# A chunked retention followed by a bilinear layer: the first tile's output by seven products for eight, and a new order of supply

## The chip, the cores and the metric

The kernel runs on one core of one Trainium2 chip. The metric is the device time of one execution in microseconds, and less is better. Engines are named as in the profile: PE (TensorE, matmul), DVE (VectorE), ACT (ScalarE), POOL (GpSimd) and SP (SyncE, which here issues nearly all transfers). L561 is line 561 of the kernel.

## The reference

```python
# q, k, v: [4, 8, 768, 64] float32; w_a, w_b: [512, 1536]; w_out: [1536, 512]
gamma = 1.0 - 2.0 ** (-5.0 - np.arange(H))
state = zeros(B, H, D, D)
for t in range(S):
    state = gamma * state + einsum('bhd,bhe->bhde', k[:, :, t], v[:, :, t])
    y[:, :, t] = (1 / sqrt(D)) * einsum('bhd,bhde->bhe', q[:, :, t], state)
x = y.transpose(0, 2, 1, 3).reshape(3072, 512)
out = ((x @ w_a) * (x @ w_b)) @ w_out          # [3072, 512] float32
```

So an attention without softmax, with a decay per head, feeds a layer with two input matrices, a product of their results, and an output matrix.

## The kernel before

**Slots.** The 4 x 768 tokens are cut into 24 chunks of 128 tokens, called slots 0 to 23. For each slot K, Q and V of all 8 heads are loaded as float32 (`load_slot`, L94; `load_two`, L99, brings Q of two slots at once), K and Q are scaled by a decay table into bfloat16 (`scaled`, L239), V is cast (`cast`, L204 and L206), and K and Q are transposed by a DMA that writes kqT (L254). `casts(t)` does all of this for slot t on POOL, with the transpose and the loads of slot t + 2 issued behind it on SP; for slots 12 to 19 V is cast by ACT (`v_cast`). The raw tiles kf, qf, vf have three buffers each, kqT has three. Slots 0 to 5 go two at a time in another form (`scores2`, `inter2`, `intra2`, `leave2`) and are transposed by PE (`tp`, L375). `turn(new, old)` computes scores, state and output of two slots and writes the layer's input xt.

**Tiles.** The layer works on tiles of 4, 2, 2, 2, 2, 4 and 8 slots (0 to 6; tile 6 is called BIG). For a tile J and one of 12 blocks ft of 128 hidden columns, `ffn_ab(J, ft)` computes a (L462) and g (L472) on PE; ACT copies a, and DVE multiplies (L474) into `ht`. The banks of PSUM for this (`psff`, tag "ff") are three.

**Output, two forms.** `ffn_out` takes one row of 128 tokens: 12 matmuls of 512 columns (L493). It is used for the four rows of tile 0 alone. All other tiles use `Group`: two rows of tokens by the two halves of the 512 output columns, as 2 x 2 blocks, with seven block products in place of eight (p1 to p7, each six matmuls of 256 columns, L561). For it one needs four sums of `ht` (`hsum(J, s, a, b)`: sum s = 1 to 4, columns a to b of six) and four of the output weights (T1 to T4, `weight_sums`). Sum 2 uses sum 3, and sum 4 uses sum 2; p6 uses sum 2, p7 sum 3, p5 sum 1, p3 sum 4. All sums are L503, whichever engine does them. `single(J)` runs the group of tile J with the first three blocks of tile J + 1 between its products: p1 p7 p2, block 0, p6, block 1, p5, block 2, p3 p4. Tile 6 also takes its a and g by seven products, for which `weight_pieces` makes sums of w_a and w_b in small pieces on POOL.

**Order.** Every instruction goes through `seq`, which keeps each engine in the order of the program text. The order is written out by hand at the end of the kernel; nothing is planned by a tool. A wait of one instruction therefore holds all that follows on its engine and on its DMA queue. `LOADS` gives the order of the first loads: pairs of slots (p), weights a and b (w), K, Q and V of the third pair, the output weights (o), and then whole slots (s).

The program up to the first group, and the third and fifth stage, shortened:

```python
    casts(6); blocks(1, 0, 3); casts(7); blocks(1, 3, NFT)
    outs(0, 0); weight_sums(0, 3); weight_sums(3, 6); outs(0, 1); casts(8); outs(0, 2)
...
    hsums(3, 0, 3, G_); casts(15); blocks(3, 9, 10); turn(12, 10); blocks(3, 10, NFT)
    hsums(3, 3, 6, G_); casts(16); single(3, Y0, AT0, FF); casts(17)
...
    casts(22); blocks(5, 6, 9); casts(23); weight_pieces(1); turn(20, 18); sums(5, 8, G_)
    blocks(5, 9, NFT); turn(22, 20); sums(5, NFT - 1, G_); weight_pieces(16); big()
```

Of the kernel before, what the change touches and what calls it, by code (L numbers as in the profile page):

```python
# [9 lines left out]
F32 = mybir.dt.float32  # L10
BF16 = mybir.dt.bfloat16
AF = mybir.ActivationFunctionType
ALU = mybir.AluOpType
# [3 lines left out]
PAIRS = 3  # L17


LOADS = "p0 p1 w0 w1 w2 w3 w4 k2 q2 a5 v2 b5 o0 o1 o2 o3 o4 o5 s6 s7".split()  # L20


@with_exitstack
def kernel(
# [55 lines left out]

    raws, wst, whole = {}, {}, {}

    def load_slot(t):
        b, ci = divmod(t, NCH)
        for nm, src in (("k", k), ("q", q), ("v", v)):
# [8 lines left out]
            seq(nc.sync.dma_start(out=raws[nm, t], in_=s))  # L94

    def load_two(nm, src, b, u, t):
        f = raw.tile([P, H, 2, D], F32, tag=nm + "f", name=nm + "f")
# [26 lines left out]
    def issue_loads(n):  # L124
        for _ in range(min(n, len(pending))):
            what = pending.pop(0)
            n = int(what[1:])
            if what[0] in "ab":
                load_w(n, what[0])
            elif what[0] in "kqv":  # L130
                load_two(what[0], {"k": k, "q": q, "v": v}[what[0]], 0, n, 2 * n)
            else:
                {"p": load_pair, "s": load_slot, "w": load_w, "o": load_o}[what[0]](n)


    kqb = {}
# [65 lines left out]
    def cast(engine, dst, src):  # L202
        if engine is nc.scalar:
            seq(nc.scalar.copy(dst, src))  # L204
        else:
            seq(engine.tensor_copy(dst, src))  # L206

    def cast_w(j, names="ab"):
        sl = slice(j * WC, (j + 1) * WC)
        for nm, dst in (("a", wa_bf), ("b", wb_bf)):  # L210
            if nm in names:
                cast(nc.gpsimd, dst[:, :, sl], wst[nm, j])

    def cast_o(j):
        cast(nc.gpsimd, wo_bf[:, j * FPO : (j + 1) * FPO, :], wst["o", j])
# [30 lines left out]
    def casts(t):  # L246
        new_nat(t)
        scaled(nc.gpsimd, t, 0)
        scaled(nc.gpsimd, t, 1)
        if t not in range(12, 20):  # L250
            cast(nc.gpsimd, vb[t], raws["v", t])
        if t % 2 == 0:
            kqT[t // 2] = tra.tile([P, 2, 2, HP, P], BF16, tag="kqT", name="kqT", bufs=3)
        seq(nc.sync.dma_start_transpose(  # L254
            out=kqT[t // 2][:, t % 2].rearrange("p a b c -> p (a b) c"),
            in_=kqb[t].rearrange("p a hp r d -> p (a hp r d)")))
        if t + 2 < NSLOT:
            load_slot(t + 2)

    def half(i):  # L260
        return slice(64 * i, 64 * i + 64)
# [183 lines left out]
    def warm(pool, tag, *cols):  # L445
        idle = pool.tile([P, HP * P], F32, tag=tag, name="idle")
        for n in cols:
            seq(nc.tensor.matmul(idle[:, :n], zero[:, :P], zero[:, :n], start=True, stop=True,  # L448
                                 skip_group_check=True))
# [30 lines left out]

    held = []

    def store():
        for dst, src in held:
            seq(nc.sync.dma_start(out=dst, in_=src))
        held.clear()

    def ffn_out(J, i):
        store()
        osb = osbp.tile([P, DM], F32, tag="osb", name="osb")  # L490
        o = psff.tile([P, DM], F32, tag="ff", name="o")
        for ft in range(NFT):
            seq(nc.tensor.matmul(o, ht[J][:, ft, i * P : (i + 1) * P], wo_bf[:, ft],  # L493
                                 start=(ft == 0), stop=(ft == NFT - 1)))
        cast(nc.scalar, osb, o)
        held.append((rows(J, i // 2, i % 2), osb))

    def rows(J, u, r):
        n0 = (sum(TILES[:J]) + 2 * u) * P
        return out[n0 : n0 + 2 * P, :].rearrange("(n r) d -> r n d", r=2)[r]  # L500

    def tt(dst, x, y, op, eng=nc.vector):
        seq(eng.tensor_tensor(dst, x, y, op=op))  # L503

    T1 = []

    def weight_sums(a, b):
        if not T1:
            T1.append(wstage.tile([P, NP, DH], BF16, tag="w", name="wsum1"))
        j = slice(a, b)  # L510
        tt(T3[:, j], B22[:, j], B12[:, j], ALU.subtract)
        tt(T2[:, j], T3[:, j], B11[:, j], ALU.add)
        tt(T4[:, j], B21[:, j], T2[:, j], ALU.subtract)
        tt(T1[0][:, j], B12[:, j], B11[:, j], ALU.subtract)

    hs = {}

    def hsum(J, s, a, b, eng=nc.vector):
        U = 2 if isinstance(J, tuple) else TILES[J] // 2
        if (J, s) not in hs:  # L520
            pool, tag = (raw, ("kf", "qf", "vf", "kf")[s - 1]) if J == (BIG, 1) else (wstage, "w")
            hs[J, s] = pool.tile([P, NP, 2, P], BF16, tag=tag, name=f"hs{s}")
        v = ht[J].rearrange("p (k j) (u r n) -> p r k j u n", k=2, r=2, n=P)
        A11, A12, A21, A22 = (v[:, r, k2, a:b, :U] for r in range(2) for k2 in range(2))
        S = {x: hs[J, x][:, a:b, :U] for x in (1, 2, 3, 4) if (J, x) in hs}
        x, y, op = {3: (A11, A21, ALU.subtract), 2: (A22, S[3], ALU.subtract), 1: (A21, A22, ALU.add),
                    4: (A12, S.get(2), ALU.subtract)}[s]
        tt(S[s], x, y, op, eng)

    def hsums(J, a, b, eng):  # L530
        for s in (2, 1, 4):
            hsum(J, s, a, b, eng)
# [300 lines left out]
    ffn_a(0, 0, 0, W2)  # L833
    intra2(1, 1, False)
    leave2(1, (A_, D_))
    ffn_a(0, 1, 0, W2)
    issue_loads(100)
    cast_w(1)
    update2(1, 1)
    ffn_a(0, 0, W2, 2 * W2)  # L840
    ffn_a(0, 1, W2, 2 * W2)
    ffn_g(0, 0, 0, W2)
# [25 lines left out]
    intra2(2, 1, False)  # L868
    leave2(2, (A_, D_))
    ffn_g(0, 10)  # L870
    ffn_g(0, 11)
    for j in range(NO):
# [12 lines left out]
    def outs(J, *rows):  # L885
        for i in rows:
            ffn_out(J, i)
# [51 lines left out]
    v_cast(14)  # L939
    blocks(4, 3, 5)  # L940
    v_cast(15)
    blocks(4, 5, 6)
    turn(14, 12)
    hsum(4, 3, 0, 6, G_)
    blocks(4, 6, 8)
    v_cast(16)
    blocks(4, 8, 9)
    hsums(4, 0, 3, G_)
    casts(18)
    blocks(4, 9, 10)  # L950
    v_cast(17)
    blocks(4, 10, 11)
    turn(16, 14)
    blocks(4, 11, NFT)
    hsums(4, 3, 6, G_)
    casts(19)
    single(4, Y0, AT0, FF)
    casts(20)
# [12 lines left out]
    sums(5, 8, G_)  # L971
    blocks(5, 9, NFT)
    turn(22, 20)
    sums(5, NFT - 1, G_)
    weight_pieces(16)
    big()


# [28 lines left out]
```

## Time and profile before

| what | value |
|---|---|
| time, median of 3 runs | 222.55 us (222.44 to 222.66) |
| the profiled execution | 222.53 us |
| its span | 220.8 us |
| PE busy | 214.2 us (97%) |
| POOL busy | 140.6 us (64%) |
| DVE busy | 135.8 us (61%) |
| ACT busy | 99.2 us (45%) |
| bytes moved by DMA | 39.68 MB |

The span is what the hardware profiler recorded between the first and the last instruction; the 1.73 us beside it lie around it. A row of a timeline gives start and length in microseconds, engine, line, operation, the tile written and the tiles read, their shape, and how many instructions the row holds; brackets give the idle time before it and what ended it. SPq stands for the DMA queue's issues on SP; a row of it is the time for which the issue held the queue. Durations of matmuls overlap the next by a little, since their ends are modelled, so products are timed here from start to start.

### The profile page before, as it was taken

The page shows a single profiled execution, that of the slowest core. Times are in us where ns is not written, and L with a number is a line of the kernel's source. Part 1 is how long each engine was busy: PE and PEld are TensorE (multiplying, and loading weights), DVE is VectorE, ACT ScalarE, POOL GpSimd, SP SyncE. Part 2 cuts the span into 40 slices and gives each one's busy share as a digit, 9 for nine tenths or more (in the row PEclk, how much of TensorE's full clock was granted, in tenths as well). Part 3 has the DMA queues.
Part 4 walks back from the last instruction along what each step waited for, and adds up shares of the span by engine and source line. Part 5 has one row for each costly group of instructions (what it writes and reads, how often), then busy time and mean ns, then how long its engine had stood idle before and what let it go on. Part 6 is the DMA issues. An engine that isn't in the chain of part 4 may idle for free.

```text
span 220.8 us, 5622 instructions
## 1 busy us (share of the span) xinstructions
PE 214.2 (97%) x2233; PEld 144.6 (66%) x2244; DVE 135.8 (61%) x254; ACT 99.2 (45%) x217; POOL 140.6 (64%) x155
## 2 busy tenths in 40 slices
PE   7999999999999999999999999999999999999994
PEld 3567445587458878878888665456865444448883
DVE  3785347745774473566476345776465777789642
ACT  3364333443224444354576344555536656542331
POOL 5364666777554469659846944599999999820000
PEclk9999999999999999999999999999999999999999
DMA  6999999997999999999998599990022000000055
GB/s 170 290 324 348 350 309 342 385 262 164 217 186 286 214 239 240 237 180 274 188 224 219 118 245 194 225 174 3 3 85 105 0 1 3 0 1 4 24 190 166
DMA packets 87194, 39.68 MB, mean 180 GB/s; under 512 B 57472, under 2 KB 82944, under 8 KB 87168
## 3 DMA queue, kind: packets, MB, share of 16 engines
q1 hardware_dynamic: 87024, 39.26, 76.9%
q8 instruction: 17, 0.28, 0.5%
q14 instruction: 9, 0.07, 0.1%
q10 hardware_dynamic: 144, 0.07, 0.1%
HBM read 28.31 MB, written 6.29 MB: 157 GB/s over the span
## 4 chain that ended last, share of the span: by engine, by line
PE 93%; DMA 2%; DVE 2%; issue 1%; ACT 0%; SPq 0%; DVEq 0%; ACTq 0%
PE a L462 19%; PE g L472 19%; PE mA L561 12%; PE uA L698 8%; PE mB L561 6%; PE o L493 5%; PE uB L698 4%; PE mC L561 3%; DMA qf<-in_q_dram 2%; PE at L273 2%; PE y L320 2%; PE uC L698 2%; PE st L290 2%; PE kb L756 2%; PE ka L756 2%; PE y L427 1%
## 5 line engine op out<-in xcount | busy, mean ns | idle before, releaser
L474 DVE TENSOR_TENSOR ht<-g,asb 128x256 bf16<-128x256 f32 (+1 forms) x74 | 37.1, 503 | 40.4 <-PE g L472 34.0
L472 PE MATMUL g<-xt,wb_bf 128*128 128x256 bf16 (+1 forms) x296 | 53.2, 304 | 0.4 <-DVE ht L474 0.4
L462 PE MATMUL a<-xt,wa_bf 128*128 128x256 bf16 (+1 forms) x292 | 53.4, 304 | 0.2
L465 ACT CAST asb<-a 128x256 bf16<-128x256 f32 (+1 forms) x74 | 32.2, 437 | 44.6 <-PE a L462 42.0
L472 PEld LDWEIGHTS <-wb_bf 128*128 128x128 bf16 x296 | 28.8, 98 | 13.4 <-issue 0.7
L239 POOL TENSOR_TENSOR kqb<-kf,ktab 128x512 bf16<-128x512 f32 x22 | 23.2, 1057 | 20.4 <-DMA kf<-in_k_dram 17.3
L462 PEld LDWEIGHTS <-wa_bf 128*128 128x128 bf16 x296 | 27.9, 98 | 12.2 <-issue 0.8
L561 PEld LDWEIGHTS <-hs 128*128 128x128 bf16 x240 | 23.4, 98 | 3.9
L279 DVE TENSOR_TENSOR aT<-at,mask 128x512 bf16<-128x512 f32 x36 | 22.3, 683 | 0.3
L704 ACT COPY snap<-uA 128x512 f32<-128x512 f32 x30 | 16.7, 588 | 12.6 <-PE uA L698 12.0
L239 POOL TENSOR_TENSOR kqb<-qf,qtab 128x512 bf16<-128x512 f32 x18 | 19.2, 1066 | 4.7 <-DMA qf<-in_q_dram 4.7
L503 POOL TENSOR_TENSOR hs<-ht,hs 128x384 bf16<-128x384 bf16 (+1 forms) x17 | 16.6, 982 | 5.8 <-DVE ht L474 5.8
L568 ACT COPY snaps<-mA 128x256 f32<-128x256 f32 x30 | 11.2, 373 | 19.8 <-PE mA L561 19.7
L561 PEld LDWEIGHTS <-ht 128*128 128x128 bf16 x180 | 17.5, 98 | 2.8
L503 POOL TENSOR_TENSOR hs<-ht 128x384 bf16<-128x384 bf16 (+2 forms) x12 | 13.8, 1152 | 3.7 <-DVE ht L474 3.7
L561 PE MATMUL mA<-wsum,hs 128*128 128x256 bf16 x120 | 15.7, 273 | 0.0
L206 POOL CAST vb<-vf 128x512 bf16<-128x512 f32 x16 | 10.1, 643 | 7.3 <-DMA vf<-in_v_dram 7.1
L503 POOL TENSOR_TENSOR ht<-gsb,asb 128x512 bf16<-128x512 bf16 x12 | 13.9, 1169 | 1.3 <-DVE gsb L503 1.3
L503 DVE TENSOR_TENSOR osb<-mB,snaps 128x256 f32<-128x256 f32 x20 | 8.4, 422 | 9.4 <-PE mB L561 5.1
L493 PE MATMUL o<-wo_bf,ht 128*128 128x512 bf16 x46 | 10.6, 380 | 0.1
L331 ACT CAST xt<-y 128x512 bf16<-128x512 f32 x18 | 9.7, 588 | 1.5 <-PE y L320 1.4
L448 PE MATMUL idle<-zero 128*128 128x256 f32 (+2 forms) x16 | 8.2, 632 | 1.6 <-DVE zero L140 1.5
(104 smaller groups left out, 323.0 us busy)
## 6 DMA issues: line engine op xcount, KB each, us to landing
qf<-in_q_dram SPq DMA_DIRECT2D x12, 512.0 KB, 5.7
out_dram<-osb SPq DMA_DIRECT2D x21, 256.0 KB, 3.9
kf<-in_k_dram SPq DMA_DIRECT2D x18, 256.0 KB, 4.6
vf<-in_v_dram SPq DMA_DIRECT2D x18, 256.0 KB, 5.4
wsta<-in_moe_w_a_dram SPq DMA_DIRECT2D x6, 512.0 KB, 8.4
wstb<-in_moe_w_b_dram SPq DMA_DIRECT2D x6, 512.0 KB, 8.1
wsto<-in_moe_w_out_dram SPq DMA_DIRECT2D x6, 512.0 KB, 7.6
kf<-in_k_dram SPq DMA_DIRECT2D x3, 512.0 KB, 7.1
```

What stands on the lines that cost most here:

```text
L239: seq(eng.tensor_tensor(dst, src, tab, op=ALU.mult))
L279: seq(nc.vector.tensor_tensor(aT[t][:, r], at[r], mask.to_broadcast([P, HP, P]), op=ALU.mult))
L462: seq(nc.tensor.matmul(a, wa_bf[:, kt, fs], xcols(J, kt, c0, c1), start=(kt == 0), stop=(kt == KT - 1)))
L465: seq(nc.scalar.copy(asb, a))
L472: seq(nc.tensor.matmul(g, wb_bf[:, kt, fs], xcols(J, kt, c0, c1), start=(kt == 0), stop=(kt == KT - 1)))
L474: seq(nc.vector.tensor_tensor(ht[J][:, ft, c0:c1], g, asbs.pop((J, ft, c0)), op=ALU.mult))
L493: seq(nc.tensor.matmul(o, ht[J][:, ft, i * P : (i + 1) * P], wo_bf[:, ft], start=(ft == 0), stop=(ft == NFT - 1)))
L503: seq(eng.tensor_tensor(dst, x, y, op=op))
L561: seq(nc.tensor.matmul(m, w, right[:, j], start=(first and j == 0), stop=(j == NP - 1), skip_group_check=True))
L568: seq(nc.scalar.copy(self.snaps[:, n], self.bank["A"]))
L698: seq(nc.tensor.matmul(m, w, right[:, k], start=(first and k == 0), stop=(k == 1), skip_group_check=True))
L704: seq(nc.scalar.copy(self.snaps[n], self.bank["A"]))
```

## The change

- Tile 0's output is taken by two `Group`s, interleaved with each other, in place of four `ffn_out`. The sums of tile 0's `ht` are made on DVE in pieces of two of six columns: some behind blocks 5, 6, 8, 10 and 11 of tile 0, and 18 parts (`todo`), of `ht` and of the weights, one behind each of the blocks 0 to 8 of tile 1 and the rest between the groups' products. The buffers are raw tiles of kf, qf and vf, and one of kqT. The groups now stand between block 8 and block 9 of tile 1.
- Sum 3 and half of sum 2 of tile 1 move to POOL.
- The start: two half blocks of a of tile 0 in place of matmuls on zeros; the casts of the first two weight pieces come in halves; state update and first g block come earlier.
- Loads: output weights in the order in which the groups use them; slots 6 and 7 as k6, q6, k7, v6, v7. `casts_two(6)` scales and transposes both slots before it casts V, and the loads of 8 and 9 follow together.
- From slot 15 on, casts stand earlier among the sums on POOL: casts(15) ahead of the first three sums of tile 3, casts(17) between sum 2 and sum 1 of its second half; in the same way 18, 19, 20 for tile 4.
- Twelve weight pieces stand ahead of casts(22) and casts(23), four ahead of the sums of tile 5, eight behind them; the pieces are in a new order.

```diff
-LOADS = "p0 p1 w0 w1 w2 w3 w4 k2 q2 a5 v2 b5 o0 o1 o2 o3 o4 o5 s6 s7".split()
+LOADS = "p0 p1 w0 w1 w2 w3 w4 k2 q2 a5 v2 b5 o0 o3 o1 o4 o2 o5 s6".split()
...
+    def load_slots(t):
+        for u, names in ((t, "kq"), (t + 1, "k"), (t, "v"), (t + 1, "v")):
+            load_slot(u, names)
...
+    def casts_two(t):
+        for u in (t, t + 1):
+            new_nat(u)
+            scaled(nc.gpsimd, u, 0)
+            scaled(nc.gpsimd, u, 1)
+            flip(u)
+        for u in (t, t + 1):
+            cast(nc.gpsimd, vb[u], raws["v", u])
+        load_slots(t + 2)
...
-    for a, b in ((0, 1), (1, 3), (3, 5)):
-        pieces += [(w, n, a, b) for w, n in (("a", 3), ("a", 2), ("b", 3), ("b", 2), ("a", 1), ("b", 1),
-                                             ("a", 4), ("b", 4))]
+    FIRST = [("a", 3), ("a", 2), ("b", 3), ("b", 2), ("a", 1), ("b", 1)]
+    LAST = [("a", 4), ("b", 4)]
+    for cols, sums_of in (((0, 1), FIRST), ((1, 3), FIRST), ((0, 1), LAST), ((1, 3), LAST),
+                          ((3, 5), FIRST + LAST)):
+        pieces += [(w, n, *cols) for w, n in sums_of]
...
-    cast_w(0)
+    cast_w(0, parts=2)
     W2 = 2 * P
-    warm(psff, "ff", 256)
+    ffn_a(0, 0, 0, W2)
+    ffn_a(0, 1, 0, W2)
...
+        if ft in (5, 6):
+            hsum(0, 3, 2 * ft - 10, 2 * ft - 8)
+        if ft == 8:
+            hsum(0, 3, 4, 6)
+            hsum(0, 2, 0, 2)
...
     ffn_g(0, 10)
+    hsum(0, 2, 2, 4)
+    hsum(0, 1, 0, 2)
     ffn_g(0, 11)
+    hsum(0, 4, 0, 2)
...
-    casts(6)
-    blocks(1, 0, 3)
-    casts(7)
-    blocks(1, 3, NFT)
-    outs(0, 0)
-    weight_sums(0, 3)
-    weight_sums(3, 6)
-    outs(0, 1)
+    todo = ("S224 T302 S124 T324 T202 T346 T224 T246 T102 T124 T146 S246 S146 S424 S446 "
+            "T402 T424 T446").split()
...
+    casts_two(6)
+    for ft in range(9):
+        ffn_ab(1, ft)
+        part()
+    hsum(1, 3, 0, 6, G_)
+    hsum(1, 2, 0, 3, G_)
+    g = [Group(0, 0, Y0, AT0, FF), Group(0, 1, Y1, AT1, FF)]
+    for x in "a1 - - b1 - - a2 - a7 - a6 - b6 - b7 - a5 b5 b2 a3 b3 a4 b4".split():
+        if x == "-":
+            part()
+        else:
+            getattr(g["ab".index(x[0])], "p" + x[1])()
     casts(8)
-    outs(0, 2)
-    turn(6, None, V_)
-    hsum(1, 3, 0, 6)
-    hsums(1, 0, 6, V_)
-    outs(0, 3)
+    store(2)
+    turn(6, None)
+    for ft in range(9, NFT):
+        ffn_a(1, ft)
+    for ft in range(9, NFT):
+        ffn_g(1, ft)
+    hsum(1, 1, 0, 3)
+    hsum(1, 4, 0, 3)
     casts(9)
     turn(None, 6)
+    hsums(1, 3, 6, V_)
     single(1, AT0, AT1, FF)
...
+    casts(15)
     hsums(3, 0, 3, G_)
-    casts(15)
     blocks(3, 9, 10)
     turn(12, 10)
     blocks(3, 10, NFT)
-    hsums(3, 3, 6, G_)
     casts(16)
+    hsum(3, 2, 3, 6, G_)
+    casts(17)
+    hsum(3, 1, 3, 6, G_)
+    hsum(3, 4, 3, 6, G_)
     single(3, Y0, AT0, FF)
-    casts(17)
...
     v_cast(19)
+    weight_pieces(12)
     blocks(5, 5, 6)
     turn(18, 16)
     sums(5, 5)
     casts(22)
+    casts(23)
     blocks(5, 6, 9)
-    casts(23)
-    weight_pieces(1)
+    weight_pieces(4)
     turn(20, 18)
     sums(5, 8, G_)
     blocks(5, 9, NFT)
     turn(22, 20)
     sums(5, NFT - 1, G_)
-    weight_pieces(16)
+    weight_pieces(8)
     big()
```

More of the change, by code (lines that the diff above doesn't have):

```diff
@@ L81, with load_slot @@
     raws, wst, whole = {}, {}, {}
-    def load_slot(t):
+    def load_slot(t, names="kqv"):
         b, ci = divmod(t, NCH)
-        for nm, src in (("k", k), ("q", q), ("v", v)):
+        for nm in names:
+            src = {"k": k, "q": q, "v": v}[nm]
             if nm == "q":
@@ L132, in issue_loads @@
             else:
-                {"p": load_pair, "s": load_slot, "w": load_w, "o": load_o}[what[0]](n)
+                {"p": load_pair, "s": load_slots, "w": load_w, "o": load_o}[what[0]](n)
     kqb = {}
@@ L206, in cast, with cast_w @@
             seq(engine.tensor_copy(dst, src))
-    def cast_w(j, names="ab"):
-        sl = slice(j * WC, (j + 1) * WC)
+    def cast_w(j, names="ab", parts=1):
+        n = WC // parts
         for nm, dst in (("a", wa_bf), ("b", wb_bf)):
-            if nm in names:
-                cast(nc.gpsimd, dst[:, :, sl], wst[nm, j])
+            for i in range(parts if nm in names else 0):
+                c = j * WC + i * n
+                cast(nc.gpsimd, dst[:, :, c : c + n], wst[nm, j][:, :, i * n : (i + 1) * n])
     def cast_o(j):
@@ L251, in casts, with flip @@
             cast(nc.gpsimd, vb[t], raws["v", t])
+        flip(t)
+        if t + 2 < NSLOT:
+            load_slot(t + 2)
+    def flip(t):
         if t % 2 == 0:
@@ L256, in casts @@
             in_=kqb[t].rearrange("p a hp r d -> p (a hp r d)")))
-        if t + 2 < NSLOT:
-            load_slot(t + 2)
+    def casts_two(t):
[7 more added lines that the diff above has]
+        load_slots(t + 2)
     def half(i):
@@ L481, with store @@
     held = []
-    def store():
-        for dst, src in held:
+    def store(n=None):
+        for dst, src in held[:n]:
             seq(nc.sync.dma_start(out=dst, in_=src))
[L486 to L496, printed above, removed]
+        del held[:n]
     def rows(J, u, r):
@@ L505, with weight_sum @@
     T1 = []
-    def weight_sums(a, b):
-        if not T1:
+    def weight_sum(n, a, b):
+        if n == 1 and not T1:
             T1.append(wstage.tile([P, NP, DH], BF16, tag="w", name="wsum1"))
         j = slice(a, b)
[L511 to L514, printed above, removed]
+        x, y, op = {3: (B22, B12, ALU.subtract), 2: (T3, B11, ALU.add), 4: (B21, T2, ALU.subtract),
+                    1: (B12, B11, ALU.subtract)}[n]
+        tt({1: T1[0] if T1 else None, 2: T2, 3: T3, 4: T4}[n][:, j], x[:, j], y[:, j], op)
     hs = {}
@@ L520, in hsum @@
         if (J, s) not in hs:
-            pool, tag = (raw, ("kf", "qf", "vf", "kf")[s - 1]) if J == (BIG, 1) else (wstage, "w")
-            hs[J, s] = pool.tile([P, NP, 2, P], BF16, tag=tag, name=f"hs{s}")
+            pool, tag = (raw, ("kf", "qf", "vf", "kf")[s - 1]) if J in (0, (BIG, 1)) else (wstage, "w")
+            if (J, s) == (0, 4):
+                pool, tag = tra, "kqT"
+            bufs = {"bufs": 3} if pool is tra else {}
+            hs[J, s] = pool.tile([P, NP, 2, P], BF16, tag=tag, name=f"hs{s}", **bufs)
         v = ht[J].rearrange("p (k j) (u r n) -> p r k j u n", k=2, r=2, n=P)
@@ L827 @@
     update2(1, 0)
-    cast_w(0)
+    cast_w(0, parts=2)
     W2 = 2 * P
-    warm(psff, "ff", 256)
+    ffn_a(0, 0, 0, W2)
+    ffn_a(0, 1, 0, W2)
     intra2(1, 0, True)
     inter2(1)
-    ffn_a(0, 0, 0, W2)
     intra2(1, 1, False)
     leave2(1, (A_, D_))
-    ffn_a(0, 1, 0, W2)
+    update2(1, 1)
+    ffn_g(0, 0, 0, W2)
     issue_loads(100)
-    cast_w(1)
-    update2(1, 1)
+    cast_w(1, parts=2)
     ffn_a(0, 0, W2, 2 * W2)
     ffn_a(0, 1, W2, 2 * W2)
-    ffn_g(0, 0, 0, W2)
     ffn_g(0, 1, 0, W2)
@@ L870 @@
     ffn_g(0, 10)
+    hsum(0, 2, 2, 4)
+    hsum(0, 1, 0, 2)
     ffn_g(0, 11)
-    for j in range(NO):
+    hsum(0, 4, 0, 2)
+    for j in (0, 3, 1, 4, 2, 5):
         cast_o(j)
@@ L883, in v_cast, with part @@
         cast(nc.scalar, vb[t], raws["v", t])
-    def outs(J, *rows):
-        for i in rows:
-            ffn_out(J, i)
-    casts(6)
-    blocks(1, 0, 3)
-    casts(7)
-    blocks(1, 3, NFT)
-    outs(0, 0)
-    weight_sums(0, 3)
-    weight_sums(3, 6)
-    outs(0, 1)
-    casts(8)
-    outs(0, 2)
-    turn(6, None, V_)
-    hsum(1, 3, 0, 6)
-    hsums(1, 0, 6, V_)
-    outs(0, 3)
+    todo = ("S224 T302 S124 T324 T202 T346 T224 T246 T102 T124 T146 S246 S146 S424 S446 "
+            "T402 T424 T446").split()
+    def part():
+        what = todo.pop(0)
+        n, x, y = map(int, what[1:])
+        if what[0] == "S":
+            hsum(0, n, x, y)
+        else:
+            weight_sum(n, x, y)
+    casts_two(6)
[8 more added lines that the diff above has]
+            part()
+        else:
+            getattr(g["ab".index(x[0])], "p" + x[1])()
+    casts(8)
+    store(2)
[6 more added lines that the diff above has]
+    hsum(1, 4, 0, 3)
     casts(9)
     turn(None, 6)
+    hsums(1, 3, 6, V_)
     single(1, AT0, AT1, FF)
@@ L943 @@
     turn(14, 12)
+    casts(18)
     hsum(4, 3, 0, 6, G_)
@@ L946 @@
     v_cast(16)
+    casts(19)
     blocks(4, 8, 9)
     hsums(4, 0, 3, G_)
-    casts(18)
     blocks(4, 9, 10)
@@ L954 @@
     blocks(4, 11, NFT)
-    hsums(4, 3, 6, G_)
-    casts(19)
+    hsum(4, 2, 3, 6, G_)
+    casts(20)
+    hsum(4, 1, 3, 6, G_)
+    hsum(4, 4, 3, 6, G_)
     single(4, Y0, AT0, FF)
-    casts(20)
     v_cast(18)
```

## The prediction

> **What bounds the kernel now.** I read the page first, then what TensorE waits for, then single stretches of each engine's timeline. The page's lines:
>
> ```profile
> span 220.8 us, 5622 instructions
> ...
> PE 214.2 (97%) x2233; PEld 144.6 (66%) x2244; DVE 135.8 (61%) x254; ACT 99.2 (45%) x217; POOL 140.6 (64%) x155
> ...
> PEclk9999999999999999999999999999999999999999
> DMA  6999999997999999999998599990022000000055
> ```
>
> TensorE is busy for 97% of the span at full granted clock. Two things follow. Fewer matmul columns are worth their full time. And there is no slack for any new wait of TensorE: it lengthens the span by its own size. The DMA row shows the other resource that is full: from 5 us to about 115 us the sixteen engines are nearly always busy. The waits of TensorE in the whole execution (us in total, times, longest) are:
>
> ```profile
> PE idle L448 <- DVE zero L140: 1.5, 1, 1.5
> PE tp L375 <- DVE kqb L239: 0.5, 2, 0.3
> PE g L472 <- DVE ht L474: 0.4, 1, 0.4
> ```
>
> So little is there to be won from waits (2.4 us, of which 1.5 us is the start). The change must win by columns, and it can lose by every operand that comes late.
>
> **Tile 0's output.** Four rows of 12 products of 512 columns become two groups of 7 x 6 products of 256 columns (TensorE's timeline: start, us, what):
>
> ```profile
> 53.73 7.93 PE L493 MATMUL o<-wo_bf,ht 128*128 128x512 bf16 x35
> 61.59 0.32 PE L290 MATMUL st<-vb,kqb 128*64 128x64 bf16 x8
> 62.77 2.76 PE L493 MATMUL o<-wo_bf,ht 128*128 128x512 bf16 x11
> 65.46 0.31 PE L310 MATMUL y<-kqT,gst 64*64 64x128 bf16 x8
> 66.27 0.83 PE L561 MATMUL mA<-wo_bf,ht 128*128 128x256 bf16 x6
> 66.93 0.82 PE L561 MATMUL mB<-wsum,hs 128*128 128x256 bf16 x6
> ```
>
> The old form takes 61.59 - 53.73 = 7.86 and 65.46 - 62.77 = 2.69, together 10.55 us. A group of six products starts 0.66 after the one before it (66.27, 66.93), so 14 of them take 9.2 us. Saved: **1.4 us**. That is all the change can gain on TensorE in this part; everything else is waiting moved about.
>
> **The sums for it.** The groups need four sums of tile 0's hidden values and four of the weights; all go to VectorE, a part of them after the last blocks of tile 0, the others one after each block of tile 1. The rows of VectorE in those places, two of TensorE, and the same shape of sum later on:
>
> ```profile
> 36.29 0.69 DVE L206 COPY kqT<-tp 128x1024 bf16<-128x1024 bf16 x1
> 37.25 0.64 PE L384 MATMUL at<-kqT 64*64 64x128 bf16 x32
> 43.38 0.69 DVE L474 TENSOR_TENSOR ht<-g,asb 128x512 bf16<-128x512 f32 x1 [0.17 <-PE g L472]
> 44.13 0.60 PE L462 MATMUL a<-xt,wa_bf 128*128 128x256 bf16 x4
> 139.40 0.41 DVE L503 TENSOR_TENSOR hs<-ht 128x512 bf16<-128x512 bf16 x1
> 140.58 0.53 DVE L503 TENSOR_TENSOR hs<-ht 128x512 bf16<-128x512 bf16 x1
> ```
>
> A sum of 128x512 is 0.41 to 0.53. Two of them now stand ahead of the copy of kqT (36.29), behind the product of block 8. The copy ends at 36.98 now and 0.8 to 1.1 later then; the scores at 37.25 have 0.27 of slack, so TensorE waits 0.5 to 0.8: I take 0.55. Two more stand between the products of blocks 10 and 11. The product at 43.38 ends at 44.07 and moves by about 0.9; the second and third products of tile 1, at 44.13 and after, need the bank that it frees, and there is 0.3 to 0.4 of room: 0.55. The 18 parts inside tile 1 come one to a block; VectorE is busy half of that time and they fit, but for about 0.2 at the first group. Together **+1.3 us**, bounds 0.3 (covered by reordering at the banks) and 2.2. POOL reads the same memory in these stretches. [...] The 0.53 against 0.41 above is as much of it as this shape shows.
>
> **The start.** The last matmuls on zeros become two half blocks of tile 0, and the weight casts come in halves. It can bring products forward by 0.3 us, but K of unit 2 is cast and turned only when its load has landed, and that order of loads is unchanged up to there: the gain ends in that wait. 0, bounds -0.3 and +0.3.
>
> **The third stage: slot 17 ahead of two sums.** Here the order on POOL changes from "three sums, casts of 15, three sums, casts of 16, group, casts of 17" to "casts of 15, three sums, casts of 16, S2, casts of 17, S1, S4, group". The second half of S1 is what the fourth product of p5 of single(3) reads. The rows of POOL, of the queue of SyncE, and p5 (the third row of PE below):
>
> ```profile
> 96.16 1.64 POOL L503 TENSOR_TENSOR hs<-ht 128x768 bf16<-128x768 bf16 x1 [1.66 <-DVE ht L474]
> 104.30 0.92 POOL L503 TENSOR_TENSOR hs<-ht 128x384 bf16<-128x384 bf16 x1
> 109.08 1.04 POOL L239 TENSOR_TENSOR kqb<-kf,ktab 128x512 bf16<-128x512 f32 x1 [1.00 <-PE g L472]
> 98.76 1.36 SPq L94 DMA_DIRECT2D vf<-in_v_dram  x1
> 100.24 3.21 SPq L485 DMA_DIRECT2D out_dram<-osb  x2
> 103.54 1.29 SPq L254 DMA_TRANSPOSE kqT<-kqb  x1
> 104.88 0.57 SPq L94 DMA_DIRECT2D kf<-in_k_dram  x1
> 106.88 0.82 PE L561 MATMUL mA<-wsum,hs 128*128 128x256 bf16 x6
> ```
>
> In the tile view of kf, that one load (issued at 104.88) has this line:
>
> ```profile
> DMA to landing us min/median/max: 4.1/4.1/4.1
> ```
>
> So K of slot 17 lands at 109.0, and POOL takes it at 109.08; the page's other name for the end of that idle time is only the last semaphore seen. Does the load come sooner in the changed kernel? It stands behind the transpose of slot 15 on SP's queue. POOL now finishes slot 15 at 97.8 + 2 x 1.0 = 99.8, ahead of three sums instead of behind them, but the queue issues slot 16's loads and two stores until 103.45 either way, held back by the full DMA engines (two stores take 3.21, where an issue alone takes 0.6). So 103.54, and 109.0, stay to within half a microsecond. Then K and Q of slot 17 and S1: 109.08 + 1.0 + 1.04 + 0.91 = 112.0. The fourth of p5's products would start at 106.88 + 0.33 = 107.2. TensorE waits 4.8 us; half a microsecond of earlier supply, from the faster first stages, makes it 4.3. I take **4.5**. Without any wait for the load of slot 17 POOL alone would need, from 97.8, six scalings of 1.0 (slots 15, 16, 17), four sums of 0.9 and S1's 0.9: 97.8 + 6.0 + 3.6 + 0.9 = 108.3, so 1.1 us at least. Bounds 1.1 and 5.0.
>
> **The fourth stage** makes the same exchange with slots 18 to 20, but there the loads have been issued before and TensorE comes 4.5 us later: 0.
>
> **The fifth stage: 12 weight pieces ahead of slots 22 and 23.** The sixth piece needs the buffer that ScalarE's cast of V of slot 19 frees. The order on POOL behind it is: this piece, six of 512, casts of 22 and 23, four pieces, then the sums of tile 5; its sixth sum is read in p6 of the first group of the big tile.
>
> ```profile
> 134.22 0.62 ACT L204 CAST vb<-vf 128x512 bf16<-128x512 f32 x1
> 143.50 1.04 POOL L239 TENSOR_TENSOR kqb<-kf,ktab 128x512 bf16<-128x512 f32 x1 [1.92 <-DMA kf<-in_k_dram]
> 146.05 0.67 POOL L503 TENSOR_TENSOR wsa<-wa_bf 128x256 bf16<-128x256 bf16 x1
> 146.68 1.15 POOL L503 TENSOR_TENSOR hs<-ht 128x512 bf16<-128x512 bf16 x1
> 153.35 1.15 POOL L503 TENSOR_TENSOR hs<-ht 128x512 bf16<-128x512 bf16 x1
> 166.63 1.15 POOL L503 TENSOR_TENSOR wsa<-wa_bf 128x512 bf16<-128x512 bf16 x1
> 154.76 0.82 PE L561 MATMUL mA<-wsum,hs 128*128 128x256 bf16 x6
> ```
>
> From start to start: a slot's three casts 2.55 (143.50 to 146.05), a small piece 0.63 (146.05 to 146.68), six sums 6.67 (146.68 to 153.35), so 1.11 for one, and a large piece, whose row has the same 1.15, as much. The chain from 134.84: 0.63 + 6 x 1.11 + 2 x 2.55 + (2 x 0.63 + 2 x 1.11) + 6.67 = 22.5, so the sixth sum ends at 157.4. p6 starts at 154.76 and its fifth product at 155.2. Today the sum is ready at 153.4. TensorE waits 2.2, and up to 0.5 more where VectorE's work slows the pieces: **+2.6**, bounds 0.5 (POOL catches up while TensorE loses time behind that cast) and 3.5. The pieces that go to the end lie under the big tile's first products.
>
> **The sum.** The profiled execution took 222.53 us, 1.73 around its span of 220.8, and the median of the three is 222.55. 222.53 - 1.4 + 1.3 + 0 + 4.5 + 2.6 = 229.5, and 0.1 for p3 behind the late S4 of stage three: **229.6 us**. A measurement of this kernel can tell about 0.2% from no change, which is 0.45 us.
>
> **The rivals.**
> *Only one sum is late.* If the supply of slot 17 runs two or three microseconds ahead, stage three costs 1.1 to 2, and if the pieces find POOL idle enough, stage five costs nothing. With one of the two as forecast and the other at its lower bound: 222.53 - 1.4 + 1.3 + 1.1 + 2.6 = 226.1, or with 4.5 + 0.5 instead 227.4. For it speaks that the first stage issues loads of two slots together; against it that the queue of SP was full from 90 to 103 for its own reasons. Chance 0.17.
> *Faster: the supply wins.* All casts come sooner, K of slot 17 lands before 104 and both late sums vanish; tile 0's sums hide behind waits that are already there. Then only the columns count: 222.53 - 1.4 = 221.1. It decides at S1's end before 107.2 and the sixth sum's before 155.2. Against it stands that POOL's own work ends S1 at 108.3 without any load. Chance 0.06; that the early loss just eats the gain and no sum is late, 0.02 (222.5).
> *A cold restart.* After a wait of 4.5 us TensorE might run slowly for a while, as at its start:
>
> ```profile
> 1.52 4.63 PE L448 MATMUL idle<-zero 128*128 128x512 f32 x6 [1.52 <-DVE zero L140]
> 10.26 1.12 PE L448 MATMUL idle<-zero 128*128 128x512 f32 x2
> ```
>
> The first 1280 columns of zeros took 4.63; at the pace of the later 512 columns in 1.12 they would be 2.8. So 1.8 us more, 231.4. No wait as long occurs later in this trace, so it is not seen what one does. Chance 0.2. [...]
>
> **How the numbers follow.** Both sums late and no cold clock: 0.55, 229.6. With a cold restart 0.2, 231.4. One sum only 0.17, around 226.8. Faster 0.06, none 0.02. The range leaves out the last two and the tails of bounds at both sides: 225.2 to 232.0. Faster by over 0.2%: 0.06; within: 0.02; slower: 0.92.
>
> **What would show it.** In the trace after: two L561 groups with 14 runs in place of L493 early on; TensorE idle for over 4 us inside p5 of single(3), named by POOL's hs, with K of slot 17 landing at about 109; a second idle stretch of 2 to 3 us at p6 before the big tile's second half. I am wrong if the load of slot 17 lands before 106, or if POOL's sixth sum of tile 5 ends before TensorE comes to it.

## The result, and the profile after

The changed kernel takes **237.27 us** (median of 5 runs, 237.09 to 238.06) against 222.52 us; the ratio is 1.0668, 95% interval 1.0649 to 1.0687. It is slower, as forecast, but by 14.8 us and not by 7.1, and outside the range. The profiled execution took 237.44 us with a span of 235.6. From the page of the kernel after:

```profile
span 235.6 us, 5717 instructions
...
PE 216.4 (92%) x2269; PEld 148.8 (63%) x2278; DVE 152.1 (65%) x277; ACT 100.3 (43%) x222; POOL 144.7 (61%) x161
...
PEclk9999999999999999999799999998899999999999
```

TensorE's share of the span fell from 97% to 92%, and the granted clock has two dents. What TensorE waited for in the kernel after (total, times, longest):

```profile
PE mA L572 <- POOL hs L512: 5.1, 1, 5.1
PE at L292 <- DMA kqT<-kqb: 2.3, 1, 2.3
...
PE mA L572 <- DVE hs L512: 1.4, 1, 1.4
PE a L481 <- DVE ht L493: 1.1, 3, 0.5
...
PE g L491 <- ACT asb L484: 0.7, 1, 0.7
```

Where the time went is read best from the starts of the same products in both timelines (us; p1 of each group, and the start of the last product):

| kernel | single(1) | single(2) | single(3) | single(4) | big, first | big, second | last product | span |
|---|---|---|---|---|---|---|---|---|
| before | 66.27 | 83.92 | 102.52 | 121.19 | 151.72 | 157.09 | 216.75 | 220.8 |
| after | 69.61 | 87.27 | 105.86 | 131.33 | 165.15 | 171.19 | 230.85 | 235.6 |
| later by | 3.34 | 3.35 | 3.34 | 10.14 | 13.43 | 14.10 | 14.10 | 14.8 |

So there are four losses: 3.3 us before single(1), 6.8 in single(3), 4.0 around the start of the big tile, and 0.7 behind the last product. Nothing is lost or won between them.

**Before single(1)**, timeline of the kernel after:

```profile
46.12 0.95 DVE L512 TENSOR_TENSOR hs<-ht,hs 128x512 bf16<-128x512 bf16 x1
47.32 1.19 DVE L512 TENSOR_TENSOR wsum<-wo_bf 128x512 bf16<-128x512 bf16 x1
50.02 0.41 DVE L512 TENSOR_TENSOR wsum<-wo_bf 128x512 bf16<-128x512 bf16 x1
45.75 1.04 POOL L211 CAST wo_bf<-wsto 128x1024 bf16<-128x1024 f32 x1 [0.17 <-DMA wsto<-in_moe_w_out_dram]
47.19 1.04 POOL L211 CAST wo_bf<-wsto 128x1024 bf16<-128x1024 f32 x1 [0.41 <-DMA wsto<-in_moe_w_out_dram]
47.45 0.60 PE L481 MATMUL a<-xt,wa_bf 128*128 128x256 bf16 x4 [0.51 <-DVE ht L493]
58.69 1.05 PE L572 MATMUL mA<-wsum,hs 128*128 128x256 bf16 x8 [1.42 <-DVE hs L512]
```

A sum of this shape takes 0.41 us when POOL is between two instructions, and 0.95 to 1.19 when it meets one of POOL's casts; the two longest rows here end 0.28 us after the cast that they meet (47.07 behind 46.79, 48.51 behind 48.23). The 18 parts take 14.8 us together, where 0.41 to 0.53 for each would be 7.4 to 9.5. With such sums VectorE is busy without a gap from 45 to 60 us; the blocks of tile 1 wait for its products, and the groups wait once more for a sum.

**In single(3)**, timeline of the kernel after:

```profile
108.23 0.91 POOL L512 TENSOR_TENSOR hs<-ht,hs 128x384 bf16<-128x384 bf16 x1
113.06 1.04 POOL L245 TENSOR_TENSOR kqb<-kf,ktab 128x512 bf16<-128x512 f32 x1 [3.92 <-issue]
115.06 0.91 POOL L512 TENSOR_TENSOR hs<-ht 128x384 bf16<-128x384 bf16 x1
103.29 2.26 SPq L504 DMA_DIRECT2D out_dram<-osb  x2
105.64 2.95 SPq L265 DMA_TRANSPOSE kqT<-kqb  x1
108.65 0.57 SPq L95 DMA_DIRECT2D kf<-in_k_dram  x1
110.41 0.49 PE L572 MATMUL mA<-wsum,hs 128*128 128x256 bf16 x3
116.03 0.82 PE L572 MATMUL mA<-wsum,hs 128*128 128x256 bf16 x3 [5.13 <-POOL hs L512]
116.64 1.06 PE L481 MATMUL a<-xt,wa_bf 128*128 128x256 bf16 x4
119.87 0.60 PE L481 MATMUL a<-xt,wa_bf 128*128 128x256 bf16 x4
```

In the tile view of kf, the load issued at 108.65 has this line:

```profile
DMA to landing us min/median/max: 4.3/4.3/4.3
```

So POOL is done with S2 at 109.1 and stands idle for 3.92 us until K of slot 17 lands at about 113.0; the word "issue" in the row means that the profile names no cause. That load left SP's queue at 108.65, behind two stores and a transpose. S1 follows at 115.06, and p5's last three products at 116.03. Behind the wait the next block takes 1.06 us for what takes 0.60 three us later.

**At the big tile**, windows (us, busy times of PE, PEld, DVE, ACT and POOL, granted clock third from the end; the first row lies behind the wait in single(3)) and timeline of the kernel after:

```profile
115.00:120.00 5.00, 3.97 (x25) 2.99 (x26) 0.85 (x2) 1.33 (x4) 3.88 (x5) 0.66 1.21 247
160.00:165.00 5.00, 2.67 (x75) 2.02 (x72) 2.44 (x4) 0.59 (x2) 5.00 (x5) 0.81 0.11 21
```

```profile
155.39 3.79 SPq L265 DMA_TRANSPOSE kqT<-kqb  x2
162.79 0.79 PE L292 MATMUL at<-kqT 64*64 64x128 bf16 x32 [2.33 <-DMA kqT<-kqb]
168.86 0.82 PE L572 MATMUL mA<-wsum,hs 128*128 128x256 bf16 x6
166.35 2.25 POOL L512 TENSOR_TENSOR hs<-ht,hs 128x512 bf16<-128x512 bf16 x2
```

The transposes of slots 22 and 23, which wait for casts behind twelve weight pieces, leave at 155.39 and after; the turn waits 2.33 us for the second, and the clock is below full here too. p6 at 168.86 does not wait: the sixth sum of tile 5, the second in the last row, ends at 168.60.

### The profile page after: what moved, and what is told of

Same layout as the page of the kernel before. It is cut to its first block, busy times and chain, and to the rows that moved or that the text cites. A ratio compares the mean times of both kernels' runs of the same rounds, so it can differ in the third digit from the quotient of the medians.

```text
span 235.6 us, 5717 instructions
## 1 busy us (share of the span) xinstructions
PE 216.4 (92%) x2269; PEld 148.8 (63%) x2278; DVE 152.1 (65%) x277; ACT 100.3 (43%) x222; POOL 144.7 (61%) x161
## 4 chain that ended last, share of the span: by engine, by line
PE 65%; DMA 10%; POOL 7%; DVE 7%; SPq 5%; issue 4%; ACT 1%; DVEq 0%; POOLq 0%; ACTq 0%
PE mA L572 13%; PE a L481 10%; PE g L491 9%; PE uA L711 7%; PE mB L572 6%; DMA qf<-in_q_dram 4%; DMA wstb<-in_moe_w_b_dram 4%; PE uB L711 4%; SPq L104 4%; PE mC L572 3%; POOL kqb L245 3%; DMA kqT<-kqb 2%; DVE ht L493 2%; DVE hs L512 2%; DVE wsum L512 2%
## 5 line engine op out<-in xcount | busy, mean ns | idle before, releaser
L572 PEld LDWEIGHTS <-hs 128*128 128x128 bf16 x288 | 28.1, 99 | 12.0 <-POOL hs L512 5.7
L579 ACT COPY snaps<-mA 128x256 f32<-128x256 f32 x36 | 13.4, 373 | 31.9 <-PE mA L572 31.8
L572 PE MATMUL mA<-wsum,hs 128*128 128x256 bf16 x144 | 19.5, 276 | 6.6 <-POOL hs L512 5.1
L572 PEld LDWEIGHTS <-ht 128*128 128x128 bf16 x216 | 21.3, 99 | 3.6 <-issue 0.2
L512 POOL TENSOR_TENSOR hs<-ht,hs 128x384 bf16<-128x384 bf16 (+1 forms) x18 | 17.6, 979 | 5.4 <-DVE ht L493 5.3
L512 DVE TENSOR_TENSOR osb<-mB,snaps 128x256 f32<-128x256 f32 x24 | 9.9, 420 | 16.2 <-ACT snaps L579 9.9
L512 POOL TENSOR_TENSOR hs<-ht 128x384 bf16<-128x384 bf16 (+2 forms) x13 | 15.6, 1199 | 7.4 <-DVE ht L493 7.4
L512 DVE TENSOR_TENSOR hs<-ht,hs 128x512 bf16<-128x512 bf16 (+2 forms) x15 | 11.4, 772 | 0.0
L512 DVE TENSOR_TENSOR hs<-ht 128x512 bf16<-128x512 bf16 (+2 forms) x15 | 11.4, 761 | 0.0
```

Source lines behind the costliest of these rows:

```text
L572: seq(nc.tensor.matmul(m, w, right[:, j], start=(first and j == 0), stop=(j == NP - 1), skip_group_check=True))
L579: seq(nc.scalar.copy(self.snaps[:, n], self.bank["A"]))
```

## The experiments

All are compared with the kernel before, run beside them on the same chip; the kernels run only twice have 95% intervals of 0.3 to 1.2% to either side, so what is said of them rests on the timelines.

**1. The third stage put back.**

```diff
-    hsum(3, 2, 3, 6, G_)
-    casts(17)
-    hsum(3, 1, 3, 6, G_)
-    hsum(3, 4, 3, 6, G_)
+    hsums(3, 3, 6, G_)
+    casts(17)
```

> The changed kernel with one thing put back: S1 and S4 of the second half of tile 3 stand ahead of the casts of slot 17 on POOL again. Theory (a late operand costs its wait and a slow restart of TensorE after it): the wait of 5.1 us in p5 of single(3) goes, and with it the slow stretch at 115 to 120 us (1.7 us), 237.3 - 6.8 = 230.5 us, and the granted clock is 1.00 there. Rival (the slow stretch has a cause of its own, or the time returns in the fifth stage since POOL's and the queues' work is no shorter): 232.2 with the slow stretch left, 233 to 235 if the fifth stage's wait grows.

Measured 233.36 us (232.29 to 234.42), 2.9 above the theory. Single(3) starts at 105.94 as in the kernel after, single(4) at 124.61 and not 131.33: the 6.7 us are gone, and the dent in the clock there with them (1.00 from 105 to 125 us). But a wait of 1.1 us appears in single(4), and the last turn still waits, so part of it is given back. The theory holds for the place; what it missed is that the fourth stage's own exchange had been covered. The two runs are 2.1 us apart; only the faster one has a trace, so that difference stays open.

**2. The fifth stage put back.**

```diff
     v_cast(19)
-    weight_pieces(12)
...
     casts(22)
-    casts(23)
     blocks(5, 6, 9)
-    weight_pieces(4)
+    casts(23)
+    weight_pieces(1)
...
-    weight_pieces(8)
+    weight_pieces(16)
```

> The changed kernel with the weight pieces of the fifth stage put back behind the casts of slots 22 and 23 (1 and 16 of them). Theory: the wait of 2.3 us for the transpose of slot 23 ahead of the last turn goes, and the slow stretch behind it (1.5 us): 237.3 - 3.9 = 233.4 us. Rival: the sums of tile 5 or the pieces become late instead at the big tile, 235 to 237.

Measured 232.53 us (232.35 to 232.72), 0.9 below the theory; in this execution the wait in single(3) was 4.3 us and not 5.1. From single(4) at 130.60 to the big tile at 161.14 are 30.54 us, as in the kernel before (30.53), where the kernel after needs 33.82. The new order of pieces and casts was the whole of that loss.

**3. Both put back.**

> Both put back. Theory: the two losses add up, 237.3 - 6.8 - 3.9 = 226.6 us, granted clock 1.00 throughout, and what is left against the kernel before is the 3.3 us lost before the first group of tile 1, and 0.7 at the end. Rival (a common bound on POOL behind both): 229 or more.

Measured 228.27 us (227.63 to 228.92), 1.7 above the expectation. In the timeline of this kernel the fourth stage shows what TensorE's lateness had hidden:

```profile
132.52 0.50 PE L572 MATMUL mA<-wsum,hs 128*128 128x256 bf16 x3 [1.38 <-POOL hs L512]
```

**4. Tile 0's output in the old form, all else new.** `ffn_out` and its order come back in place of the two groups and the 18 parts.

> The changed kernel with tile 0's output in the old form of eight products, with the old places of its sums of weights and of tile 1's sums, and all else new. Theory (the sums of tile 0 fill VectorE from 44 to 63 us and cost 4.7 us for 1.4 us of columns saved): 237.3 - 3.3 = 234.0 us. Rival (the early loss comes from the loads of slots two at a time or from the start): 236 to 238.

Measured 233.24 us (232.9 to 233.57), 0.8 below the theory. Single(1) starts at 66.05, 0.2 us ahead of the kernel before: the early loss is that of tile 0's form, and the start and the paired loads gain 0.2. In this execution the last turn waited only 0.6 us, and the wait came at p6 instead:

```profile
166.19 0.39 PE L572 MATMUL mA<-wsum,hs 128*128 128x256 bf16 x2 [2.41 <-POOL hs L512]
```

**5. The fourth stage put back as well**: `hsums(4, 3, 6, G_)` ahead of `casts(20)`, beside the edits of 1 and 2.

> As the run with the third and fifth stage put back, and the fourth stage's S1 and S4 of the second half of tile 4 also ahead of the casts of slot 20. In that run TensorE waits 1.4 us in p5 of single(4), a wait that is absent in the changed kernel, where TensorE comes 5 us later. Theory (the exchange costs a wait in the fourth stage too, once the third no longer hides it): 1.4 to 1.6 us less, 226.0 to 226.7 us, no wait for a POOL sum over 0.5 us. Rival (POOL is behind from the third stage on for another reason): the wait stays at 1.0 to 1.4.

Measured 227.54 us (226.79 to 228.3), 0.8 above the theory's range; the profiled execution took 226.79. No wait for a POOL sum is left from single(1) on, and from single(1) at 69.67 to the big tile at 155.22 are 85.55 us against 85.45 before.

**6. And tile 0 in the old form.**

> The same with tile 0's output in the old form as well: of the change only the start, the order and pairing of the first loads, and the earlier places of slots 15, 18, 19 are left. Theory (all of the loss is in four places: tile 0's sums on VectorE and the three late operands): 222.3 us, level with the kernel before or 0.2 us faster, as single(1) started 0.2 us earlier in the run with only tile 0 put back. Rival (loads in pairs cost something by themselves): 223 or more.

Measured 222.40 us (222.09 to 222.51, 10 runs) against 222.49; ratio 0.9991, interval 0.9981 to 1.0001: no difference that can be told, and so, within that interval, the four edits undone here were the whole loss.

**7. POOL's casts of the output weights in four pieces**, on top of 5.

```diff
-        cast(nc.gpsimd, wo_bf[:, j * FPO : (j + 1) * FPO, :], wst["o", j])
+        for i in range(FPO):
+            for c in range(0, DM, 256):
+                cast(nc.gpsimd, wo_bf[:, j * FPO + i, c : c + 256], wst["o", j][:, i, c : c + 256])
```

> As the run with stages three to five put back, with POOL's casts of the output weights cut in four: 24 of 128x256 in place of 6 of 128x1024, the same work in shorter instructions. [...]

In 5 the four sums between 44 and 49.5 us take 0.84 to 1.26 us, and each ends 0.27 to 0.29 us after the POOL instruction of 1.04 us that it meets. If that instruction sets their length, shorter casts make shorter sums. Timeline of this kernel:

```profile
46.07 0.62 DVE L514 TENSOR_TENSOR hs<-ht,hs 128x512 bf16<-128x512 bf16 x1
46.95 0.62 DVE L514 TENSOR_TENSOR wsum<-wo_bf 128x512 bf16<-128x512 bf16 x1
47.83 0.62 DVE L514 TENSOR_TENSOR hs<-ht 128x512 bf16<-128x512 bf16 x1
40.23 9.70 POOL L211 CAST wo_bf<-wsto 128x256 bf16<-128x256 f32 x24 [0.27 <-DMA wsto<-in_moe_w_out_dram]
58.26 1.89 PE L574 MATMUL mA<-wsum,hs 128*128 128x256 bf16 x8 [2.40 <-DVE hs L514]
```

The sums fall to 0.62 although POOL is now busy without a gap, with 24 casts of 0.40 us, and the waits of blocks for ht between 43 and 55 us (0.60, 0.84 and 0.26 in 5) are gone from the timeline: tile 0's groups start at 52.65 and not 54.96. Behind the casts, beside POOL's scalings of 1.21 and 1.22 us, three sums take 0.93 again and end 0.28 to 0.29 us after the scaling that they meet. So a sum's length goes with the POOL instruction beside it, and not with POOL's share of busy time. The time is 228.77 us (227.47 to 230.08), no better, since the groups now wait 2.40 us for a sum of 1.85 us that ends 0.28 us after one of POOL of 1.80, and the clock falls to 0.50 behind that wait, from 58 to 61 us.

**8. TensorE kept busy in the wait.** `warm(psat, "y1", 512, 512, 512, 512)` ahead of p5 of single(3), in the kernel after.

> The changed kernel with four matmuls of 512 columns on zeros ahead of p5 of single(3), 4.5 us of work that nothing needs, in the place of the wait. Theory (TensorE runs slowly after the 5.1 us of idling): the wait shrinks to 0.6 to 0.8, the granted clock stays 1.00 from 115 to 120 us, and the stage is 1.5 to 1.7 us shorter although it does more work: 235.6 us. Rival (the slow stretch is not for the idling): no change in the clock there, 237 to 239.

```profile
111.02 3.60 PE L467 MATMUL idle<-zero 128*128 128x512 f32 x8
115.81 0.50 PE L572 MATMUL mA<-wsum,hs 128*128 128x256 bf16 x3 [0.86 <-POOL hs L512]
116.15 0.60 PE L481 MATMUL a<-xt,wa_bf 128*128 128x256 bf16 x4
```

235.64 us (234.89 to 236.39). The block behind p5 takes 0.60 and not 1.06, the granted clock is 1.00 throughout 114 to 121 us, and single(4) starts at 129.80, 1.5 us sooner, with 3.6 us of useless work more. So the slow stretch is the price of idling.

**9. Less on VectorE ahead of tile 0's groups**, on top of 5: one sum that was made twice dropped, six sums of tile 0 earlier, POOL's weight casts in halves, V of slots 6 and 7 cast by ScalarE.

> As the run with stages three to five put back, with less on VectorE ahead of tile 0's groups: the sum that is made twice (S224) once, six of the sums of tile 0 earlier (behind blocks 2, 4, 6, 7 and after the scores of unit 2), POOL's casts of the output weights in halves, and V of slots 6 and 7 cast by ScalarE in place of POOL. Theory (the early loss is VectorE's time, its sums lengthened by POOL's instructions): tile 0's groups start at 52.0 to 52.8 and not 55.0, wait under 0.8 us in all for sums, single(1) starts at 66.5 to 67.3 and the time is 224.0 us (223.4 to 224.8), still above the kernel before. Rival (the sums only wait elsewhere, as in the run with the casts in quarters): single(1) at 69 or later, 226 to 228.

224.20 us (223.57 to 225.73, 8 runs). The groups start at 52.61 and wait for nothing, and single(1) starts at 66.58 where 5 has 69.67: 3.1 of the early loss were VectorE's time. Which of the four edits won how much, no run separates. Single(1) is still 0.3 us later than before, and in that stretch one g block waits 0.67 for ScalarE's copy of the a block just before it, which it does not read; the kernel after has the same wait. No run shows why it waits for that copy. In this execution, the slowest of the eight, p5 of single(3) also waits 1.52 us for a POOL sum.

**10. Two stores held back** behind the loads of slot 17, in the kernel after.

> The changed kernel with the two stores of tile 2 held back until the loads of slot 17 have been issued; all else as in the changed kernel. Theory (S1 is late because K of slot 17 lands at 112.9, which is set by what stands ahead of its load on SP's queue, and POOL alone would need it 1.1 us late): the load lands 2.5 to 4 us sooner, the wait in p5 of single(3) falls from 5.1 to 1.2 to 2.6 us, and without a wait of over 2.5 us the slow stretch behind it goes: 231.7 to 234.5 us. Rival (POOL's own work is the limit): the wait stays above 4 us, 237.

```profile
110.87 1.04 POOL L245 TENSOR_TENSOR kqb<-kf,ktab 128x512 bf16<-128x512 f32 x1 [1.91 <-DMA kf<-in_k_dram]
113.84 0.66 PE L572 MATMUL mA<-wsum,hs 128*128 128x256 bf16 x3 [2.88 <-POOL hs L512]
```

234.29 us (233.51 to 235.06). K of slot 17 is there 2.2 us sooner, and the wait is 2.2 us shorter: so much of it was set by the two stores ahead of that load on SP's queue. The load left the queue 2.5 us sooner (106.14 for 108.65) and took 4.6 us to land where it took 4.3. The gain of 2.5 to 4 us and the wait of at most 2.6 were just missed, and the clock still fell, to 0.50 from 114 to 117 us. The 2.5 us above which it was to fall were the author's estimate: in 1 it fell behind a wait of 1.98.

**11 and 12. The seven products with the later stages as before.** In 11 sum 3 of tile 0 stands behind block 6 in one piece of three; 12 has the early part of 9. Both have the order of the kernel before from slot 10 on.

> The best that these runs point to: tile 0 by seven products as in the run with less on VectorE, its three pieces of sum 3 together behind block 6, and everything from slot 10 on in the order of the kernel before. [...] Theory (nothing else is left of the early loss): single(1) at 65.7 to 66.3 against 66.27, no wait of over 0.8 us in the third to fifth stage, 222.0 to 222.6 us. Rival (three sums in a row delay the product of block 7, or the later stages depend on the new supply): 223 to 224.

> The early part of the run with less on VectorE, and everything from slot 10 on in the order of the kernel before. Theory: single(1) 0.2 to 0.4 us later than in the kernel before, as in that run, nothing lost behind it, and so 222.7 to 223.1 us: with all hidden that these runs could hide, the seven products come out level or 0.1% to 0.3% slower. Rival (the later stages need the new order once tile 0 is done by seven products, since the supply is later): over 224.

11 took 225.26 us (224.89 to 226.14, ratio 1.0127), more than its theory and its rival allow, and single(1) is 2.8 us late. The g block's wait for ScalarE's copy is 0.23 us here, where 9 has 0.67. But in its timeline an a block waits for ScalarE's copy of a transposition (kqT), which is none of its operands; no run shows why:

```profile
36.24 1.02 PE L480 MATMUL a<-xt,wa_bf 128*128 128x512 bf16 x4 [1.10 <-ACT kqT L209]
```

12 took 223.79 us (223.40 to 224.15; ratio 1.0054, interval 1.0041 to 1.0066). Single(1) is 0.56 us late, and the same 0.55 to 0.57 stand at every later landmark. This missed the expectation by 0.7, and 0.7 us are lost behind the last product.

**13. Instructions alone.** In every kernel with tile 0 by seven products, the stretch from the start of the last product to the end was 4.27 to 5.41 us and the instruction queue had 18 transfers; in the three without it 4.05 to 4.10 and 17. In the kernel before:

```diff
-    warm(psat, "y1", 512, 512, 256)
+    for _ in range(36):
+        seq(nc.tensor.matmul(idle[:, :64], ident, ident[:, :64], ...))
```

> The kernel before, with the three matmuls on zeros at the start, 4.6 us long while TensorE has nothing else to do, replaced by 36 short ones of 64 columns with their weight loads: 69 more instructions for TensorE, 4555 as in the changed kernel, and the same work everywhere else. Theory (a program that is longer by so much needs an 18th transfer on the instruction queue, which falls among the last stores): 18 transfers there, the stretch from the last product's start to the end 4.6 to 5.2 us where it is 4.05 before, and the time 0.6 to 1.0 us longer, 223.1 to 223.5 us. Rival (the longer tail comes from tile 0's new form, its buffers or stores): 17 or 18 transfers, the tail at 4.05 to 4.1, and 222.3 to 222.7 us.

The queue's line on the page of the kernel before, and on that of this one:

```profile
q8 instruction: 17, 0.28, 0.5%
```

```profile
q8 instruction: 18, 0.29, 0.6%
```

The time is 224.55 us (223.72 to 225.08, ratio 1.0081), 1.0 above the theory's range. 1.0 us of the 2.5 in its span is lost at the start, where the trace's first clock record, full speed, begins at 11.8 us and not at 7.2 (two matmuls of 256 columns take 1.17 us at 8.71, two of 512 take 1.13 at 11.77; single(1) at 67.28); the other 1.5 are behind the last product, which starts at 217.75 of a span of 223.3. One store's issue near the end takes 2.0 us where the others take 0.3 to 0.4, and the 18th transfer starts in it, at 217.3:

```profile
217.27 2.03 SPq L580 DMA_DIRECT2D out_dram<-osb  x1
```

So a longer program of TensorE is enough for the longer tail, without tile 0's new form.

## Why the prediction was wrong, step by step

- **Columns, -1.4:** right within 0.2. The groups take 10.86 us in the kernel after with 1.42 us of waiting in them, so 9.4 where 9.2 was forecast.
- **The sums for tile 0, +1.3:** mis-sized, and this is the step that failed first. The start gained 0.3 (block 2 starts at 21.77 and not 22.08), but the early part with it still lost 4.7, the 3.3 and the 1.4 saved. "VectorE is busy half of that time and they fit" took 0.41 to 0.53 for a sum; ten of the 18 parts took 0.92 to 1.86, because POOL was casting the weights and slots 6 and 7 and making sums of tile 1 then. The prediction named POOL's reading beside them, gave it no term here, and read "0.53 against 0.41" as all of it. That row was only the end of such a meeting: in the rows below POOL's scaling ends at 140.82, 0.24 us after that sum's start, and the sum ends 0.29 us later; the sum of 1.19 in the kernel after starts 0.91 us before its cast ends. 9, which mends more than the lengthening, wins back 3.1; what the lengthening costs alone, no run separates. The g block's wait of 0.67 was not foreseen either.

```profile
139.78 1.04 POOL L239 TENSOR_TENSOR kqb<-qf,qtab 128x512 bf16<-128x512 f32 x1 [0.76 <-DMA qf<-in_q_dram]
140.58 0.53 DVE L503 TENSOR_TENSOR hs<-ht 128x512 bf16<-128x512 bf16 x1
```

- **Third stage, +4.5:** right in mechanism and nearly in size, 5.1: POOL waits for K of slot 17 with S1 behind it. 1 and 10 show it from two sides. The load did not stay at 109.0, though. It landed at about 113.0, as the stores ahead of it came 3.1 us later (103.29 for 100.24), and TensorE was ready for the fourth product at 110.9 and not at 107.2. Both moved alike, so the difference held.
- **Fourth stage, 0:** right in this kernel, and for the reason given: 1.4 us appear when TensorE is on time (3).
- **Fifth stage, +2.6:** right that the pieces ahead of the casts cost TensorE a wait, wrong in which. The wait of 2.33 came at the last turn, for the transpose of slot 23, which the prediction did not count. The sixth sum ended at 168.60, before p6 needed it, which is the prediction's own sign of being wrong. That 2.33 is close to 2.6 is luck, as another operand set it. The wait moves with the landing of that transpose: in 4 it was 0.6 at the turn and 2.4 at p6, for that sum.
- **The cold restart** was a rival with a chance of 0.2 for one place, and nothing in the sum. It came twice, 1.7 and 1.6 us, behind waits of 5.1 and 2.3; the price from the first row of before, 1.8, was near. The clock also fell behind the wait of 2.33 us, which is shorter than one of the clock's steps of 3.41 us. By these steps, shown in the last section, a wait of 3.96 us or more puts 1.98 us into one of them wherever it lies, which was enough in 1. So behind the forecast 4.5 us a fall was to be expected (an estimate from these traces); the trace of before could not have told it.
- **The tail, 0.7:** not foreseen; nothing in the prediction counted instructions.

The terms as measured: -1.4 + 4.7 + (5.1 + 1.7) + (2.33 + 1.63) + 0.7 = 14.8, the third and fifth stage each taken as the difference of the landmarks. The result lies 7.7 above the forecast: 3.4 for the sums of tile 0, 3.3 for the two slow restarts, 0.6 and -0.3 for the two late stages, 0.7 for the tail. Without the first two it would have been 230.6, by this sum.

## What to carry to other kernels

Cost a moved instruction by what runs beside it in its new place and not by its shortest row (a sum of one shape took 0.41 us here, and 1.19 beside a cast on POOL): count the busy time of the target engine with the longer value first. In a kernel that one engine bounds (TensorE, busy for 97% of the span before), a late operand costs its wait (5.1 us in single(3)) and can cost a slow restart (1.7 us there), so a queue order must be judged by the load that each instruction waits for, with the queue that the load itself stands in. And when several stages are changed alike, undo them one by one and together, since one late stage covers the next (1.4 us appeared in 3).

## What the runs showed of the hardware that was not expected

- Behind waits, the granted clock fell to 0.50 nine times in these traces, each time for 3.41 us, but for 6.83 in 4 behind the 5.11 us of single(3). The clock records of a trace begin where the clock first is at full speed, and the falls start a whole number of such steps after that: in the kernel after, full speed begins at 6.13 and the falls at 115.36 and 163.14, 32 and 46 steps later. Cut into these steps, the traces show what went with the falls: behind these waits, each step at full clock in which PE was idle for 1.98 us (the least, in 1) to 3.41 us was followed by a step at half clock, and steps with 1.76 (in 2) and 1.65 (in 4) were not. The wait of 2.33 us in the kernel after lay in one step (first two rows), and that of 2.41 in 4 was split into 1.65 and 0.76 over two and cost no fall (last two rows; the first busy time is PE's). Where the steps lie differs from execution to execution, as the begin of full speed does (4.8 us in 10, 11.8 in 13), so what a wait of 2 to 4 us costs is partly luck.

```profile
159.73:163.14 3.41, 1.08 (x28) 0.47 (x30) 0.69 (x1) 0.49 (x1) 3.41 (x4) 1.00 0.25 46
163.14:166.55 3.41, 3.41 (x70) 2.69 (x60) 2.48 (x4) 1.45 (x3) 3.41 (x4) 0.50 0.00 0
162.02:165.43 3.41, 1.76 (x11) 0.78 (x8) 0.11 (x1) 1.17 (x2) 3.41 (x4) 1.00 0.01 2
165.43:168.84 3.41, 2.65 (x47) 2.12 (x48) 0.30 (x1) 1.45 (x3) 3.41 (x4) 1.00 0.00 0
```

- Two transposes issued 2.6 us apart, those of slots 22 and 23 in the kernel after, landed after 3.1 and 4.8 us, and the tile view of kqT gives the spread:

```profile
DMA to landing us min/median/max: 3.1/3.9/4.8
```

- 69 more instructions for TensorE, at the start in 13 and in tile 0's groups in the kernels with the seven products, went with an 18th transfer on the instruction queue and 0.2 to 1.5 us more at the end of this kernel.
